# Local attention followed by two expert layers on one core: another order within the attention loop's steps

## Chip, core and metric

The program runs on one NeuronCore of a Trainium2 chip. TensorE (PE in the rows) does matmuls and transposes, VectorE is DVE, ScalarE is ACT, GpSimd is POOL, and SyncE (SP) issues most of the DMA transfers. Each engine works through its own queue in order and waits where an operand is not ready. The metric is the device time of one execution in microseconds; lower is better. All times below are microseconds unless they say ns.

## What is computed

Three layers stand one behind the other: attention with a local window and a few global keys, a layer in which each row goes to one of 8 experts, and a layer in which each row goes through all 4 experts, weighted. Cut to what matters:

```python
# attention: B=2, H=8, S=768, D=64, n_global=8, n_local=96
scores = q @ k.T / sqrt(D) + bias            # kept only for global keys and the last 96 positions
a = exp(scores - max(scores)); a /= sum(a) + 1e-9
x = (a @ v).reshape(1536, 512)
# first expert layer: 1 of 8 per row, chosen by the largest logit
logits = normalized(x) @ normalized(emb).T / tau
e = argmax(logits);  y = gate * (relu(x @ w1[e]) @ w2[e])
# second expert layer: all 4
out = sum_e p[:, e] * (relu(y @ v1[e]) @ v2[e])
```

## The kernel before

**Tiles and runs.** The 1536 rows are 12 tiles of 128 (index `t_`), 6 per batch element. The 8 heads of a tile are 4 pairs (index `n` runs over all tiles' pairs), and two pairs are a *run*. The attention loop makes 24 steps `s_` (line 565); step `s_` belongs to tile `s_ // 2`, its first or second run (`i` = 0 or 1). In a tile at the start of a batch element the scores are 128 columns wide, elsewhere 240.

**What a run goes through.** `scores` (4 matmuls in the program, 8 records in the trace, line 474) into two PSUM buffers, one for each head of a pair, both pairs side by side; `maximum` on VectorE (485: adds the bias in place and takes the row maximum, followed by a small read of the accumulator); `expo` on ScalarE (493: exponential into `aa`, row sum into `sums`); `flip` (501: transposes of `aa` on TensorE, then a copy to `ats`, 503, on ScalarE or VectorE); `av` (515: matmuls with the values into `o`); `fin0` (193: copy of half a tile's `o` to `os` on ScalarE); `fin_l` (210: matmuls of `os` with an identity that also holds the expert embedding, into the single PSUM buffer `l`, tile name `lp`); then on VectorE `over_sums` (229, `lh`) and `rows_x` (241, `xall`), which multiply by the reciprocal of the sums that `sum_up` makes (219 on GpSimd, 220 on VectorE).

**Routing.** When both runs of a tile are there, `choose` queues five closures with six small VectorE operations (257 to 260, 252, 253) that find the expert; `fill()` takes one closure out of that queue. `count` (269, 270) counts with two small matmuls where each row goes, `fin2` (278 to 284) turns that into a slot number, and `scatter` (289, GpSimd's DMA queue) writes the tile's rows into the DRAM buffer `xs`, which `zero_fill` (420) has set to zero in four transfers.

**Order.** The order is written out by hand: every engine executes what the Python code issues to it, in that order, and waits are put in for the data and the buffers. In step `s_` the code issues, in this order: the flips of the step's own run, `ends(s_)` (the end of run `s_ - 2`: `fin_l`, `over_sums`, `rows_x`, and after a second run `fin2` of the tile before and `choose`), `scores(s_ + 2)`, `av` of run `s_ - 1`, then maxima and exponentials of run `s_ + 2` with one `fill()` after each and `fin0` in their midst, then scatter, loads, zero rows and the first expert layer's weights (`load_to`, `split_to`).

**The end of attention.** After the loop, `scatter` of tile 9, then SP loads the first expert's rows `xe` from `xs` (622); they are turned by 16 matmuls (299, `first_rows`), the last two tiles' rows are added by `add_rows` (303) with a permutation that `fin2` makes (281), and the result is split in `x0` (650, 651). Then the first expert's matmuls start (798).

Of the kernel before, what the change touches and what calls it, by code (L numbers as in the profile page):

```python
# [34 lines left out]
def tile_attention_moe_moe(ctx: ExitStack, tc: tile.TileContext, q, k, v, n_global, n_local,  # L35
# [179 lines left out]
    def sum_up(t_):  # L215

        rs = pl.sb.tile([P, H], F32, tag="rs", name="rs")
        lh = pl.sb.tile([P, H, NE], F32, tag="lh", name="lh")
        nc.gpsimd.tensor_scalar(rs, sums[t_], 1e-9, None, ALU.add)
        nc.vector.reciprocal(rs, rs)  # L220
        osb[t_, 2] = rs, lh

    def over_sums(t_, i):
# [82 lines left out]
    with ExitStack() as at:  # L306
# [144 lines left out]

        sc, nm_, aa, ats = {}, {}, {}, {}
        NS = 2 * T

        def pairs(s_):
            return range(2 * s_, 2 * s_ + 2)
# [30 lines left out]
        def expo(n, j):  # L487
            t_, p_ = divmod(n, NP)
            w = P if t_ % TB == 0 else WIN
            if j == 0:  # L490
                aa[n] = ap4.tile([P, 2, 2 * P], F32, tag="aa", name="aa")
            h = 2 * p_ + j
            nc.scalar.activation(aa[n][:, j, 0:w], score(n, j), AF.Exp, bias=nm_[t_][:, h:h + 1], scale=-1.0,  # L493
                                 accum_out=sums[t_][:, h:h + 1])
# [29 lines left out]
        def ends(s_):  # L524

            t_, i = divmod(s_ - 2, 2)
            if t_ >= 0:
                fin_l(t_, i, place=t_ - 1 if i and t_ else None)
                if i == 0:
                    sum_up(t_)  # L530
                over_sums(t_, i)
                rows_x(t_, i)
                if i:
                    if t_:
                        fin2(t_ - 1)
                    choose(t_)

        warm(10)
        build_bias0(0)
# [6 lines left out]
        warm(4)  # L546
        for n in pairs(0):
            for j in range(2):
                maximum(n, j)
                expo(n, j)  # L550
        build_bias0(2)
        build_bias0(3)
        for n in pairs(1):
            for j in range(2):
                maximum(n, j)
                expo(n, j)
        build_biasw(0)
        build_biasw(1)
        nc.gpsimd.memset(zt, 0.0)
        nc.gpsimd.memset(idn[:, :, 2 * D:], 0.0)  # L560
        nc.gpsimd.tensor_copy(idn[:, :, 0:2 * D], ident.unsqueeze(1).to_broadcast([P, NP, P]))
# [3 lines left out]
        for s_ in range(NS):  # L565
            t_, i = divmod(s_, 2)
            n0, n1 = pairs(s_)
            flip(n0, nc.scalar.copy)
            flip(n1, nc.scalar.copy if s_ % 2 else nc.vector.tensor_copy)
            ends(s_)  # L570
            if s_ == 1:
                build_enblk2()
            if s_ == 23:
                break
            scores(s_ + 2)
            if s_ >= 1:
                for n in pairs(s_ - 1):
                    av(n)
            if s_ == 0:
                build_biasw(2)  # L580
                build_biasw(3)
                build_enblk()
            for n in pairs(s_ + 2):
                for j in range(2):
                    if n < NP * T:
                        maximum(n, j)
                        expo(n, j)
                    fill()
                    if s_ >= 1 and n % 2 == 1 and j == 0:
                        fin0((s_ - 1) // 2, (s_ - 1) % 2)  # L590
            if s_ == 1:
                put_globals(0, 1, TB - 1)
            if s_ == 2 * TB - 2:
                put_globals(1, 0, TB - 1)
            if s_ == 2:
                build_flag()
            if ready:
                scatter(ready.pop(0))
            if i == 0 and 1 <= t_ and t_ + 2 < T:
                load_v(t_ + 2)  # L600
            if i == 1 and t_ + 4 < T:
                load_kq(t_ + 4)
            if s_ == 1:
                build_tables()
            if s_ == 4:
                ci = ap1.tile([P, CAP], I32, name="ci")
                nc.gpsimd.iota(ci, [[1, CAP]], base=0, channel_multiplier=0)
                nc.gpsimd.tensor_copy(col, ci)
            if s_ < 4:
                zero_fill(s_)  # L610
            if i == 1:
                load_to(min(nxt[1] + RAW, t_))
                if t_ >= 1:
                    split_to(min(t_ - 1, PRE - 2))
            else:
                split_low(nc.gpsimd, False)


        scatter(ready.pop(0))
        xe = ap1.tile([P, 2, NP, P], F32, name="xe").rearrange("p i a n -> p i (a n)")  # L620
        for i in range(2):
            nc.sync.dma_start(out=xe[:, i], in_=xs[i * P:(i + 1) * P, :])
        for n in pairs(NS - 2):
            av(n)
        fin0(T - 1, 0)
        for n in pairs(NS - 1):
            av(n)
        fin0(T - 1, 1)
# [1 line left out]
        fin_l(T - 1, 0, place=T - 2)  # L630
        fin2(T - 2)
        scatter(ready.pop(0))
        sum_up(T - 1)
        over_sums(T - 1, 0)
        rows_x(T - 1, 0, True)
        fin_l(T - 1, 1, ps_a)
# [389 lines left out]
    with tc.If(fb > 0):  # L1026
        with ExitStack() as ge:
# [23 lines left out]
            for b in range(B):  # L1051
                og = gp.tile([P, TB, NP, P], F32, tag="og", name="og")
                sg = gp.tile([P, TB, H], F32, tag="sg", name="sg")
                for p_ in range(NP):
                    gq = gp.tile([P, TB, P], F32, tag="gq", name="gq")
                    gk = gp.tile([P, S], F32, tag="gk", name="gk")
                    gv = gp.tile([P, TB, 2 * D], F32, tag="gv", name="gv")
                    nc.sync.dma_start(out=gq, in_=q[b * TB:(b + 1) * TB, :, p_, :].rearrange("t p s -> p t s"))
                    nc.sync.dma_start(out=gk, in_=k[b, :, p_, :])
                    nc.sync.dma_start(out=gv, in_=v[b, :, p_ * 2 * D:(p_ + 1) * 2 * D].rearrange("(t s) d -> s t d", s=P))  # L1060
                    for i in range(TB):
                        po = ps_g.tile([P, P], F32, tag="po", name="po")
                        for j in range(2):
                            h = 2 * p_ + j
                            r0 = slice(64 * j, 64 * j + 64)
                            sg_ = gp.tile([P, S], F32, tag="s", name="s")
                            for f in range(2):
                                pt = ps_g.tile([P, S // 2], F32, tag=f"sc{f}", name="pt")
                                cs = slice(f * S // 2, (f + 1) * S // 2)
                                nc.tensor.matmul(pt, gq[r0, i, :], gk[r0, cs], start=True, stop=True)  # L1070
                                nc.vector.scalar_tensor_tensor(sg_[:, cs], dist[:, i, cs], -8.0 * 2.0 ** (-8.0 * (h + 1) / H), pt,
                                                               ALU.mult, ALU.add)
                            kp = keep[:, i, :]
                            nc.vector.tensor_tensor(sg_, sg_, kp, ALU.mult)
                            mk = gp.tile([P, S], F32, tag="mk", name="mk")
                            nc.vector.tensor_scalar(mk, kp, -1.0, NEG8, ALU.add, ALU.mult)
                            nc.vector.tensor_tensor(sg_, sg_, mk, ALU.add)
                            nm = gp.tile([P, 1], F32, tag="nm", name="nm")
                            nc.vector.tensor_reduce(nm, sg_, AX.X, ALU.max)
                            nc.vector.tensor_scalar(nm, nm, -0.125, None, ALU.mult)  # L1080
                            nc.scalar.activation(sg_, sg_, AF.Exp, bias=nm, scale=0.125, accum_out=sg[:, i, h:h + 1])
                            for c in range(TB):
                                pt = ps_g.tile([P, P], F32, tag="at", name="pt")
                                nc.tensor.transpose(pt, sg_[:, c * P:(c + 1) * P], ident)
                                at_ = gp.tile([P, P], F32, tag="at", name="at")
                                nc.vector.tensor_copy(at_, pt)
                                nc.tensor.matmul(po[r0, :], gv[:, c, j * D:(j + 1) * D], at_, start=c == 0, stop=c == TB - 1)
                        nc.vector.tensor_copy(og[:, i, p_, :], po)
                for i in range(TB):
                    t_ = b * TB + i  # L1090
                    sums[t_] = sg[:, i, :]
                    osb[t_] = og[:, i]
                    sum_up(t_)
                    for j in range(2):
                        fin_l(t_, j)
                        over_sums(t_, j)
                        rows_x(t_, j)
                    choose(t_)
                    fill(len(small))
# [104 lines left out]
```

## Time and profile before

| | |
|---|---|
| runs | 840.21, 841.39, 841.75 (median 841.39) |
| the profiled execution | 841.09, of which the span of the trace is 839.4 |
| busy in the span | PE 801.0 (95%), DVE 548.3 (65%), ACT 355.8 (42%), POOL 269.1 (32%) |
| attention, until the first expert's first matmul | 0 to 130.1 |
| the two expert layers | 130.1 to 839.4 |
| DMA | 77.8 MB, 93 GB/s over the span |

Read the shares stage by stage: in the expert layers TensorE is busy all the time, in attention none of the engines is. So the first question for attention is not which engine has the most work but which chain of waits closes from one step to the next. A row of the chain of waits gives start, length, engine, what it wrote and its line; a row of the timeline gives the same with shapes and, in brackets, the idle time before it and what ended it.

### The profile page before, as it was taken

The page shows a single profiled execution, that of the slowest core. Times are in us where ns is not written, and L with a number is a line of the kernel's source. Part 1 is how long each engine was busy: PE and PEld are TensorE (multiplying, and loading weights), DVE is VectorE, ACT ScalarE, POOL GpSimd, SP SyncE. Part 2 cuts the span into 40 slices and gives each one's busy share as a digit, 9 for nine tenths or more (in the row PEclk, how much of TensorE's full clock was granted, in tenths as well). Part 3 has the DMA queues.
Part 4 walks back from the last instruction along what each step waited for, and adds up shares of the span by engine and source line. Part 5 has one row for each costly group of instructions (what it writes and reads, how often), then busy time and mean ns, then how long its engine had stood idle before and what let it go on. Part 6 is the DMA issues. An engine that isn't in the chain of part 4 may idle for free.

```text
span 839.4 us, 14797 instructions
## 1 busy us (share of the span) xinstructions
PE 801.0 (95%) x5699; PEld 728.8 (87%) x5699; DVE 548.3 (65%) x1358; ACT 355.8 (42%) x733; POOL 269.1 (32%) x248
## 2 busy tenths in 40 slices
PE   7887879999999999999999999999999999999996
PEld 3675668999999998999989989989989989989995
DVE  7667745676666554555676676676676676676674
ACT  5687635775555544354233223224223223223221
POOL 3154126107000025136136136136136235235322
PEclk7999999999999999999999999999999999999998
DMA  8756313666666551001001101110110010000111
GB/s 275 270 185 234 122 64 113 218 202 209 207 205 179 195 186 66 26 26 52 26 26 36 39 27 27 36 40 26 28 50 26 27 51 26 27 1 1 51 51 54
DMA packets 32271, 77.80 MB, mean 93 GB/s; under 512 B 3960, under 2 KB 10120, under 8 KB 32192
## 3 DMA queue, kind: packets, MB, share of 16 engines
q1 hardware_dynamic: 29632, 70.36, 26.5%
q0 software_dynamic: 2416, 6.41, 2.1%
q8 instruction: 47, 0.77, 0.4%
q14 instruction: 32, 0.26, 0.1%
q10 hardware_dynamic: 144, 0.00, 0.0%
HBM read 66.22 MB, written 10.53 MB: 91 GB/s over the span
## 4 chain that ended last, share of the span: by engine, by line
PE 79%; DVE 12%; ACT 5%; issue 2%; DMA 1%; POOL 1%; SPq 0%; POOLq 0%; ACTq 0%; DVEq 0%
PE h L925 9%; PE h L924 9%; PE h L926 9%; PE z L989 8%; PE z L992 8%; PE z L991 8%; PE h L798 4%; PE h L799 4%; PE h L800 4%; PE y L814 4%; PE y L813 4%; PE y L812 4%; ACT aa L493 3%; DVE sh L960 2%; PE lp L210 2%
## 5 line engine op out<-in xcount | busy, mean ns | idle before, releaser
L895 DVE SCALAR_TENSOR_TENSOR xall<-z,rsb,xall 128x256 f32<-128x256 f32 x312 | 133.7, 477 | 35.6 <-PE z L992 35.2
L924 PE MATMUL h<-x2h,wh 128*128 128x512 f32 (+1 forms) x400 | 152.8, 382 | 0.0
L925 PE MATMUL h<-x2l,wh 128*128 128x512 f32 (+1 forms) x400 | 152.8, 382 | 0.0
L926 PE MATMUL h<-x2h,wl 128*128 128x512 f32 (+1 forms) x400 | 152.2, 381 | 0.0
L989 PE MATMUL z<-wt,sh 128*128 128x256 f32 x384 | 109.6, 286 | 4.8 <-DVE xall L895 4.8
L992 PE MATMUL z<-wt,sl 128*128 128x256 f32 x384 | 108.7, 283 | 0.7 <-DVE sl L969 0.7
L991 PE MATMUL z<-wt,sh 128*128 128x256 f32 x384 | 108.6, 283 | 0.0
L941 POOL TENSOR_TENSOR bl<-h,bh 128x512 fp32r<-128x512 f32 (+1 forms) x25 | 31.9, 1274 | 192.6 <-PE z L992 167.5
L956 ACT ACTIVATE ah<-h 128x512 fp32r<-128x512 f32 (+1 forms) x50 | 29.1, 582 | 140.6 <-PE h L926 140.6
L926 PEld LDWEIGHTS h<-x2h,wl 128*128 128x128 f32 x400 | 75.2, 188 | 14.7
L924 PEld LDWEIGHTS h<-x2h,wh 128*128 128x128 f32 x400 | 75.4, 189 | 13.2
L925 PEld LDWEIGHTS h<-x2l,wh 128*128 128x128 f32 x400 | 75.4, 189 | 13.0 <-issue 0.3
L989 PEld LDWEIGHTS z<-wt,sh 128*128 128x128 f32 x384 | 73.5, 191 | 7.7 <-DVE xall L895 6.8
L992 PEld LDWEIGHTS z<-wt,sl 128*128 128x128 f32 x384 | 73.5, 191 | 0.9 <-DVE sl L969 0.9
L991 PEld LDWEIGHTS z<-wt,sh 128*128 128x128 f32 x384 | 73.6, 192 | 0.8
L934 ACT ACTIVATE h<-h 128x512 f32<-128x512 f32 (+1 forms) x50 | 28.7, 574 | 107.3 <-PE h L926 107.3
L91 DVE TENSOR_TENSOR wl<-raw,wh 128x1024 fp32r<-128x1024 f32 x61 | 74.0, 1234 | 0.0
L812 PE MATMUL y<-hh,wh 128*128 128x256 f32 x256 | 73.2, 286 | 0.0
L814 PE MATMUL y<-hh,wl 128*128 128x256 f32 x256 | 72.0, 281 | 0.0
L813 PE MATMUL y<-hl,wh 128*128 128x256 f32 x256 | 71.9, 281 | 0.0
L110 ACT ACTIVATE wh<-raw 128x1024 fp32r<-128x1024 f32 x66 | 69.0, 1056 | 2.9 <-DMA raw<-in_moe_w_dram 2.9
L152 POOL TENSOR_TENSOR wt<-raw,wt 128x512 fp32r<-128x512 f32 x40 | 51.6, 1299 | 57.4 <-ACT wt L151 50.2
(214 smaller groups left out, 1987.5 us busy)
## 6 DMA issues: line engine op xcount, KB each, us to landing
raw<-in_moe_w_dram SPq DMA_DIRECT2D x96, 512.0 KB, 3.7
xs<-zt SPq DMA_DIRECT2D x4, 1024.0 KB, 5.8
xr<-xs SPq DMA_DIRECT2D x14, 256.0 KB, 4.0
k<-in_k_dram SPq DMA_DIRECT2D x12, 256.0 KB, 3.4
q<-in_q_dram SPq DMA_DIRECT2D x12, 256.0 KB, 5.1
v<-in_v_dram SPq DMA_DIRECT2D x12, 256.0 KB, 2.8
vwin<-in_v_dram SPq DMA_DIRECT2D x10, 192.0 KB, 4.2
xe<-xs SPq DMA_DIRECT2D x2, 256.0 KB
```

The lines of the kernel that those rows point to most:

```text
L91: eng.tensor_tensor(lo, r, hi.bitcast(F32), ALU.subtract)
L110: nc.scalar.activation(hi, r, AF.Copy)
L812: nc.tensor.matmul(y_, wh[:, f, ws], hh[:, kf, :], start=kf == 0, stop=False)
L813: nc.tensor.matmul(y_, wh[:, f, ws], hl[:, kf, :], start=False, stop=False)
L814: nc.tensor.matmul(y_, wl[:, f, ws], hh[:, kf, :], start=False, stop=kf == KF - 1)
L895: nc.vector.scalar_tensor_tensor(a_, src[:, i], w_, a_, ALU.mult, ALU.add)
L924: nc.tensor.matmul(pt, wh[:, d, ws], x2h[:, d, cs], start=d == 0, stop=False)
L925: nc.tensor.matmul(pt, wh[:, d, ws], x2l[:, d, cs], start=False, stop=False)
L926: nc.tensor.matmul(pt, wl[:, d, ws], x2h[:, d, cs], start=False, stop=d == KD - 1)
L989: nc.tensor.matmul(pt[:, i], hh[:, f, ts_], wh[:, f, :], start=o_ < 3 and i == f == 0, stop=False, skip_group_check=True)
L991: nc.tensor.matmul(pt[:, i], hh[:, f, ts_], wl[:, f, :], start=False, stop=False, skip_group_check=True)
L992: nc.tensor.matmul(pt[:, i], hl[:, f, ts_], wh[:, f, :], start=False, stop=f == 1, skip_group_check=True)
```

## The change

All of it is in the attention loop and its end.

- Within a step the order is now: maxima and exponentials of run `s_ + 1` (`top`, mixed with the flips of run `s_`), `ends(s_)`, `av` of run `s_ - 1`, `fin0`, all waiting small operations at once (`fill(len(small))`), and last `scores(s_ + 2)`. So the scores made at the end of a step are taken up in the following step.
- The flips' copies swap: ScalarE makes both in even steps, VectorE one in odd steps.
- `sum_up`'s reciprocal is issued in `ends`, its GpSimd part at the end of the odd step before.
- `count` and `fin2` of the tile before go with a tile's first run, and no longer with the second.
- Zero rows are written in steps 2, 4, 5 and 7, scatters begin in step 9, one per step while any are ready. The load of `xe` is issued in step 22, inside the loop.

```diff
@@ sum_up
-        nc.vector.reciprocal(rs, rs)
@@ ends
-                fin_l(t_, i, place=t_ - 1 if i and t_ else None)
                 if i == 0:
-                    sum_up(t_)
+                    nc.vector.reciprocal(osb[t_, 2][0], osb[t_, 2][0])
+                fin_l(t_, i, place=t_ - 1 if t_ and not i else None)
                 over_sums(t_, i)
                 rows_x(t_, i)
                 if i:
-                    if t_:
-                        fin2(t_ - 1)
                     choose(t_)
+                elif t_:
+                    fin2(t_ - 1)
+
+        def top(n, j):
+            if n < NP * T:
+                maximum(n, j)
+                expo(n, j)
@@ the loop
+            m0, m1 = pairs(s_ + 1)
+            top(m0, 0)
             flip(n0, nc.scalar.copy)
-            flip(n1, nc.scalar.copy if s_ % 2 else nc.vector.tensor_copy)
-            ends(s_)
+            top(m0, 1)
+            flip(n1, nc.vector.tensor_copy if s_ % 2 else nc.scalar.copy)
+            top(m1, 0)
+            top(m1, 1)
...
+            ends(s_)
-            scores(s_ + 2)
             if s_ >= 1:
                 for n in pairs(s_ - 1):
                     av(n)
...
-            for n in pairs(s_ + 2):
-                for j in range(2):
-                    if n < NP * T:
-                        maximum(n, j)
-                        expo(n, j)
-                    fill()
-                    if s_ >= 1 and n % 2 == 1 and j == 0:
-                        fin0((s_ - 1) // 2, (s_ - 1) % 2)
+                fin0((s_ - 1) // 2, (s_ - 1) % 2)
+            fill(len(small))
+            scores(s_ + 2)
+            if i:
+                sum_up(t_)
...
-            if ready:
+            if ready and s_ > 8:
                 scatter(ready.pop(0))
...
-            if s_ < 4:
-                zero_fill(s_)
+            if s_ in ZF:
+                zero_fill(ZF.index(s_))
...
-        scatter(ready.pop(0))
-        xe = ap1.tile([P, 2, NP, P], F32, name="xe").rearrange("p i a n -> p i (a n)")
-        for i in range(2):
-            nc.sync.dma_start(out=xe[:, i], in_=xs[i * P:(i + 1) * P, :])
-        for n in pairs(NS - 2):
-            av(n)
-        fin0(T - 1, 0)
+            if s_ == NS - 2:
+                xe = ap1.tile([P, 2, NP, P], F32, name="xe").rearrange("p i a n -> p i (a n)")
+                for c in range(2):
+                    nc.sync.dma_start(out=xe[:, c], in_=xs[c * P:(c + 1) * P, :])
```

Before the loop, maxima and exponentials of run 1 and part of the bias tables move into its first steps.

What stands in a row on ScalarE over two steps in the middle of the loop. Before (`aa` is an exponential, `ats` a flip's copy, `os` the copy of `fin0`):

```order
L493 ACTIVATE aa,sums<-s,nm 128x240
L503 COPY ats<-at 128x512 x2
L493 ACTIVATE aa,sums<-s,nm 128x240 x3
L193 COPY os<-o 128x256
L493 ACTIVATE aa,sums<-s,nm 128x240
L503 COPY ats<-at 128x512
L493 ACTIVATE aa,sums<-s,nm 128x240 x3
L193 COPY os<-o 128x256
```

The same two steps after the change, the even one first:

```order
L493 ACTIVATE aa,sums<-s,nm 128x240
L503 COPY ats<-at 128x512
L493 ACTIVATE aa,sums<-s,nm 128x240
L503 COPY ats<-at 128x512
L493 ACTIVATE aa,sums<-s,nm 128x240 x2
L193 COPY os<-o 128x256
L493 ACTIVATE aa,sums<-s,nm 128x240
L503 COPY ats<-at 128x512
L493 ACTIVATE aa,sums<-s,nm 128x240 x3
L193 COPY os<-o 128x256
```

A flip's copy now stands between the first and the second exponential of a run, and `os` behind all four.

VectorE before, from the end of `fin2` to the next reciprocal (`s,nm` with its `nm` row is one maximum, `l`, `sm`, `oh`, `ohb` are the small operations of `choose`):

```order
L485 ISA s,nm<-s,biasw 128x240
L485 ISA nm 128x1
L257 TENSOR_REDUCE l_79<-lh 128x8
L485 ISA s,nm<-s,biasw 128x240
L485 ISA nm 128x1
L258 TENSOR_REDUCE sm<-l_79 128x1
L485 ISA s,nm<-s,biasw 128x240
L485 ISA nm 128x1
L259 SCALAR_TENSOR_TENSOR sm<-l_79,sm,rev 128x8
L485 ISA s,nm<-s,biasw 128x240
L485 ISA nm 128x1
L260 TENSOR_REDUCE sm<-sm 128x1
```

VectorE after, from the last maximum of an odd step:

```order
L485 ISA s,nm<-s,biasw 128x240
L485 ISA nm 128x1
L228 TENSOR_TENSOR lh<-lp,rs 128x32
L240 TENSOR_TENSOR xall<-lp,rs 128x256
L256 TENSOR_REDUCE l_79<-lh 128x8
L257 TENSOR_REDUCE sm<-l_79 128x1
L258 SCALAR_TENSOR_TENSOR sm<-l_79,sm,rev 128x8
L259 TENSOR_REDUCE sm<-sm 128x1
L251 TENSOR_SCALAR oh<-sm 128x8
L252 CAST ohb<-oh 128x8
```

The six small operations, spread over the maxima before, now stand in one row behind `xall`, and the next step's first maximum behind them.

GpSimd's queue at the end of attention, before:

```order
L289 DMA xs<-xall,slot 2048x512
L254 TENSOR_TENSOR cum<-cum,oh 128x8
L285 TENSOR_TENSOR base<-pos 128x1
L289 DMA xs<-xall,slot 2048x512
L219 TENSOR_SCALAR rs<-sums 128x8
L254 TENSOR_TENSOR cum<-cum,oh 128x8
```

and after:

```order
L288 DMA xs<-xall,slot 2048x512
L253 TENSOR_TENSOR cum<-cum,oh 128x8
L219 TENSOR_SCALAR rs<-sums 128x8
L284 TENSOR_TENSOR base<-pos 128x1
L288 DMA xs<-xall,slot 2048x512
L253 TENSOR_TENSOR cum<-cum,oh 128x8
```

The sums `rs` of the last tile stood behind the scatter of tile 10; now they stand ahead of it.

## Rows read from the trace of the kernel before

**Rows 1.** Busy time by stretch: length, PE, PEld, DVE, ACT, POOL, PEclk, DMA share.

```profile
140.00:160.00 20.00, 20.00 (x171) 20.00 (x171) 13.49 (x21) 14.14 (x30) 9.05 (x12) 1.00 0.72 234
```

**Rows 2.** Chain of waits, 0 to 215: start, length, engine, written, line.

```profile
23.84 0.40 DVE s L485
...
82.89 0.76 PE lp L210 x4
83.65 1.06 PE s L474 x8
...
87.24 0.76 PE lp L210 x4
...
91.80 0.76 PE lp L210 x4
...
110.38 1.03 PE o L515 x16
111.40 1.02 PE at L501 x8
112.43 0.49 PE lp L210 x4
...
114.06 0.22 DVE slot L284
```

**Rows 3.** Timeline of two steps, 82 to 91.5: start, length, engine, line.

```profile
87.08 0.47 ACT L493 ACTIVATE aa<-s,nm 128x240 f32<-128x240 f32 x1
...
87.53 1.08 ACT L503 COPY ats<-at 128x512 f32<-128x512 f32 x2
...
88.11 0.19 DVE L229 TENSOR_TENSOR lh<-lp,rs 128x32 f32<-128x32 f32 x1 [1.18 <-PE lp L270]
...
88.54 0.16 DVE L278 CUSTOM_DVE_ANT_0 g<-ebase,oh 128x8 f32<-128x8 f32 x1
...
89.14 0.22 DVE L284 SCALAR_TENSOR_TENSOR slot<-pos 128x1 int32<-128x1 f32 x1
...
89.28 0.41 DVE L485 CUSTOM_DVE_ANT_0 s<-s,biasw 128x240 f32<-128x240 f32 x1
...
89.60 0.26 DVE L257 TENSOR_REDUCE l<-lh 128x8 f32<-128x64 f32 x1
...
89.84 0.46 ACT L493 ACTIVATE aa<-s,nm 128x240 f32<-128x240 f32 x1 [1.23 <-DVE nm L485]
...
90.42 0.42 DVE L485 CUSTOM_DVE_ANT_0 s<-s,biasw 128x240 f32<-128x240 f32 x1 [0.16 <-ACT aa L493]
```

**Rows 4.** Timeline of the end of attention, 104 to 132.

```profile
107.09 0.41 DVE L485 CUSTOM_DVE_ANT_0 s<-s,biasw 128x240 f32<-128x240 f32 x1
...
121.16 3.67 PE L299 MATMUL xy<-ident,xe 128*128 128x128 f32 x16 [4.29 <-DMA xe<-xs]
...
123.85 0.20 DVE L220 RECIPROCAL rs<-rs 128x8 f32<-128x8 f32 x1 [6.47 <-POOL rs L219]
124.09 0.29 DVE L229 TENSOR_TENSOR lh<-lp,rs 128x32 f32<-128x32 f32 x2
...
124.41 0.27 DVE L257 TENSOR_REDUCE l<-lh 128x8 f32<-128x64 f32 x1
...
125.72 0.42 DVE L241 TENSOR_TENSOR xall<-lp,rs 128x256 f32<-128x256 f32 x1
...
125.86 0.17 PE L269 MATMUL pp<-ohb,tri 128*128 128x8 bf16 x1 [0.16 <-DVE ohb L253]
...
130.11 0.38 PE L798 MATMUL h<-x,wh 128*128 128x256 f32 x1 [0.92 <-DVE x L651]
```

**Rows 5.** Busy time by stretch of 2 us, the columns of rows 1.

```profile
118.00:120.00 2.00, 0.00 (x0) 0.00 (x0) 0.00 (x0) 0.00 (x0) 0.00 (x0) 1.00 0.10 30
...
122.00:124.00 2.00, 2.00 (x12) 2.00 (x11) 0.15 (x1) 0.00 (x0) 1.23 (x2) 0.50 0.00 0
```

**Rows 6.** DMA issues on the page: count, KB each, median us to landing.

```profile
xs<-zt SPq DMA_DIRECT2D x4, 1024.0 KB, 5.8
```

More of the change, by code (lines that the diff above doesn't have):

```diff
@@ L453, in tile_attention_moe_moe @@
         NS = 2 * T
+        ZF = (2, 4, 5, 7)
         def pairs(s_):
@@ L548, in tile_attention_moe_moe @@
             for j in range(2):
-                maximum(n, j)
-                expo(n, j)
+                top(n, j)
         build_bias0(2)
         build_bias0(3)
-        for n in pairs(1):
-            for j in range(2):
[L555 to L558, printed above, removed]
         nc.gpsimd.memset(zt, 0.0)
@@ L567, in tile_attention_moe_moe @@
             n0, n1 = pairs(s_)
+            m0, m1 = pairs(s_ + 1)
+            top(m0, 0)
             flip(n0, nc.scalar.copy)
-            flip(n1, nc.scalar.copy if s_ % 2 else nc.vector.tensor_copy)
-            ends(s_)
+            top(m0, 1)
+            flip(n1, nc.vector.tensor_copy if s_ % 2 else nc.scalar.copy)
+            top(m1, 0)
+            top(m1, 1)
+            if s_ < 2:
+                build_biasw(2 * s_)
+                build_biasw(2 * s_ + 1)
+            if s_ == 0:
+                build_enblk()
             if s_ == 1:
                 build_enblk2()
-            if s_ == 23:
-                break
-            scores(s_ + 2)
+            ends(s_)
             if s_ >= 1:
@@ L578, in tile_attention_moe_moe @@
                     av(n)
[L579 to L582, printed above, removed]
-            for n in pairs(s_ + 2):
-                for j in range(2):
-                    if n < NP * T:
-                        maximum(n, j)
-                        expo(n, j)
-                    fill()
-                    if s_ >= 1 and n % 2 == 1 and j == 0:
-                        fin0((s_ - 1) // 2, (s_ - 1) % 2)
+                fin0((s_ - 1) // 2, (s_ - 1) % 2)
[3 more added lines that the diff above has]
+                sum_up(t_)
             if s_ == 1:
@@ L632, in tile_attention_moe_moe @@
         scatter(ready.pop(0))
-        sum_up(T - 1)
+        nc.vector.reciprocal(osb[T - 1, 2][0], osb[T - 1, 2][0])
         over_sums(T - 1, 0)
@@ L1093, in tile_attention_moe_moe @@
                     sum_up(t_)
+                    nc.vector.reciprocal(osb[t_, 2][0], osb[t_, 2][0])
                     for j in range(2):
```

## Prediction

> **What bounds the kernel now.** I read the busy time by stretch first. From 140 on TensorE is busy for the whole of a stretch at full clock [rows 1], and no instruction of the two expert layers changes. So they keep their 709 us (130.11 to 839.4), start when attention ends, and all that can be won or lost lies before the first expert's matmul at 130.11 [rows 4].
>
> The chain of waits comes next, because no engine is full in attention. In the loop it returns to the same instruction, `fin_l`'s matmuls: 82.89, 87.24, 91.80 [rows 2], which is 8.91 for a pair of steps. TensorE's own work in a step is 1.02 (transposes), 1.03 (`o`), 1.06 (`s`) and 0.49 (`lp` where it didn't have to wait) [rows 2], 3.60 in all, 7.2 for a pair, and the two small counting matmuls. So 1.5 to 1.7 of each 8.91 is waiting. The loop closes like this: `lp`, behind it the scores, from them the maxima, the exponentials, in their midst `os` on ScalarE, and `os` feeds the next `lp`. One run goes nearly all the way round in each step.
>
> The timeline gives the hand-offs that any order has to pay. From a maximum to its exponential 0.56 (89.28 to 89.84), and from that exponential to the third maximum of the run 0.58 (89.84 to 90.42), which waits for ScalarE although it belongs to another pair [rows 3]: both lie in one PSUM buffer. The fourth waits for the second exponential in the same way.
>
> **The change, part by part. The loop.** The scores of a run are now made a step before they are needed, and `lp` comes behind 1.02 of transposes, so the old ring is cut open. What ring is late next? In the new order VectorE does four maxima, then the end of an older run, then the next step's maxima. The fourth maximum needs the second exponential, and on ScalarE a flip's copy now stands between the first and the second. So I go from the first maximum of one step to that of the next, with durations from the rows:
>
> maximum to exponential 0.56; exponential to copy 0.45 (87.08 to 87.53); copy 0.54 (half of 1.08); second exponential to fourth maximum 0.58 [rows 3]. Together 2.13 in every step. The fourth maximum to the instruction behind it takes 0.32 (89.28 to 89.60).
>
> Even step, then: reciprocal to `lh` 0.24 (123.85 to 124.09) [rows 4], `lh` to `fin2` 0.43 (88.11 to 88.54), `fin2` to its `slot` 0.60, `slot` to the next maximum 0.14 [rows 3]. 2.13 + 0.32 + 0.24 + 0.43 + 0.60 + 0.14 = 3.86.
>
> Odd step: `lh` and `xall` 0.43 again, and the six small operations in one row 1.31 (124.41 to 125.72) [rows 4]. Spread over the maxima they were nearly free, here they are on the path. 2.13 + 0.32 + 0.43 + 1.31 = 4.19.
>
> A pair takes 8.05 instead of 8.91. Other rings are shorter. TensorE's work is 7.4 for a pair, counting matmuls included. The way exponential, transpose, `lp`, `o`, `s`, maximum goes over two steps: 2.13 to the fourth maximum, 0.56 and some 0.5 for the last exponential, 1.02, 0.49, 1.03 and 1.06, which is 6.8. ScalarE has four exponentials, one or two copies and `os`, some 3.5 in a step, and 1.1 more where a weight is split; that stands behind `os`, ends before the next first exponential, and so stays hidden (if not, one for one).
>
> In the odd steps VectorE's copy stands ahead of the third maximum. It costs nothing while it can start within 1.07 of the first maximum (2.13 less 0.46 and 0.54 and a little), and the transposes that it needs should be done 0.3 after it.
>
> From the first maximum of run 4 (23.84) [rows 2] to that of run 23 (107.09) [rows 4] it was 83.25 for 19 steps, 1.4 less than 19 halves of 8.91, since one tile's runs are narrow. Now it is 10 odd steps of 4.19 and 9 even ones of 3.86, 76.64; for the narrow runs I take off 1.0. 75.6, a gain of 7.6. How the hand-offs add up where they have never stood together is unknown: 0.15 less for a pair or 0.45 more, so 9.0 down to 3.3.
>
> **The first steps.** The same bias tables, maxima and copies stand on VectorE up to run 4, only in another order, and VectorE works there nearly without a break. I take 0, with 0.7 either way: below, because zero rows no longer compete with the first keys and queries; above, because copies now delay maxima.
>
> **Zero rows, scatters, loads.** Four transfers of 1 MB land 5.8 after their issue [rows 6]. SP issues the last in step 7, the first scatter waits for it in GpSimd's queue at the end of step 9, some 8 later. Behind a scatter that waits would stand `cum` and the sums `rs`, which VectorE needs at the end of step 12: another 12 of cover, then one for one. The first weights are queued behind zero rows on SP, with about 8 from issue to use; late ones would hold ScalarE. I take 0, and at most 1 lost.
>
> **The end.** The `xe` load is issued a step earlier, and what follows it is the old chain. Before, `slot` at 114.06 [rows 2], through scatter and load, led to the first turning matmul at 121.16; from there 4.70 to the counting matmul (125.86), and 4.25 to the expert's first matmul (130.11). Counted from the first maximum of run 23 at 107.09 that is 23.02 [rows 4]. Now that maximum stands in step 22, an even one, whose `slot` comes 3.86 - 0.14 = 3.72 later: 3.72 + 7.10 + 4.70 + 4.25 = 19.77. The gain is 3.25. The last run's flips, `av`, `fin0` and `lp` are done about 8 after that maximum, inside the 7.10; the last tile's expert is known at about 11, behind `rs`, which no longer waits in GpSimd's queue behind a scatter that waits for `xe` (the 6.47 of idle time at 123.85) [rows 4]. That wait was hidden behind TensorE and is not counted again.
>
> Of the 4.70, 3.67 are 16 matmuls at half clock [rows 4]: TensorE had no work from 118 to 120, with the full clock still granted (1.00), and at 122 to 124 it had 0.50, 1.2 GHz [rows 5]. At full clock the turning takes 2.04 (twice 1.02 of 8 transposes [rows 2]), and the rest a few tenths less, so the end would gain 5.2. Now TensorE will be without work for about 3 instead of 4.3. I take half clock, the nearest row. The Trainium skill, "TensorE: Matmul & The Clock Gate", section "Part 1: The HAM clock gate", says that the slow clock is the default and that only activity lifts it. By that alone every such pause ends at half clock and the time is the 830.5 below; by the row in which the clock outlasted the pause it would be 828.5.
>
> **The sum.** 7.6 + 0 + 0 + 3.25 = 10.9 off the profiled execution's 841.09 is 830.2. That execution was 0.3 under the median of 841.39, so against the runs I say 830.5.
>
> **Rivals.**
> *TensorE becomes the bound.* If the third and fourth maximum don't have to wait behind the copy, a pair takes TensorE's 7.4: 1.5 x 9.5 = 14.3, less 0.5 for narrow runs, and 3.25: 824.3. For it speaks that TensorE's share is already the largest; against it the wait of 0.16 on ScalarE that the trace shows for just this maximum [rows 3].
> *The loop doesn't open.* The step stays at 4.45 because hand-offs grow, or `lp`, of which there is one buffer, is held by a late `fin2`; only the end is won: 838.1. For it: half of the new ring is small VectorE operations, whose price is taken from two places at the end of attention. Against it: the ring is made of measured steps throughout.
> *Slower: the copy blocks VectorE.* In odd steps the copy stands in VectorE's queue ahead of the third and fourth maxima, the end of the older run and the next step's maxima. It needs the second transposes, these need the fourth exponential of the even step. If they are ready only after 1.07 from the first maximum, each 0.1 more costs 0.1 a pair, 0.95 in all; from 2.2 on the loop's and the end's gain is gone, and at 2.5 the pair costs 1.43 more than my 8.05, 13.6 in all: 844.1. Against it: by my sum the transposes are ready some 0.8 before that point. For it: such a copy at the head of an in-order queue ties all three engines together.
>
> **Chances.** Forecast, 826 to 835.5: 0.62. TensorE bound: 0.09. The loop stays, 835.5 to 839: 0.19. Slower by the copy or by late weights: 0.10. The range reaches from the forecast's lower end to most of the third case: 826 to 837. About 0.2%, 1.7 us, is what a measurement of this kernel can tell from no change. Faster by more than that 0.86, within it 0.05, slower 0.09.
>
> **What would show it.** The distance of `lp` to `lp` over two steps should be 8.0 to 8.2, odd steps 0.3 longer than even ones; the fourth maximum should wait for ScalarE, no longer the first for TensorE; TensorE should wait before the second flip for an exponential. `xe` should be issued some 8 after the first maximum of run 23, and the expert's first matmul should stand at about 119. I am wrong if the pair stays near 8.9, if maxima wait for TensorE's scores, if ScalarE waits for a weight's transfer, or if the experts take longer than 709.

## Result and profile after

| | before | after |
|---|---|---|
| median of the runs | 840.99 (840.21 to 841.75) | 833.22 (831.79 to 833.34) |
| the profiled execution, of which span | 841.09, 839.4 | 833.17, 831.5 |
| first maximum of run 4 (`maximum`) | 23.84 | 22.54 |
| first maximum of run 23 | 107.09 | 103.66 |
| first expert's first matmul | 130.11 | 122.46 |

The ratio is 0.9904 [0.9887, 0.9921]: 7.8 faster, inside the range of 826 to 837, but 2.7 short of the 830.5. By stretch, in the two profiled executions:

| stretch | forecast gain | measured gain |
|---|---|---|
| up to the first maximum of run 4 | 0 | 1.30 |
| from there to the first maximum of run 23 | 7.6 | 2.13 (83.25 to 81.12) |
| from there to the expert's first matmul | 3.25 | 4.22 (23.02 to 18.80) |
| the expert layers | 0 | 0.3 |
| sum | 10.9 | 7.9 |

So the total came nearer than its terms, partly by luck: the loop lost 5.5 of what it should have won, and two stretches gave back 2.3 unasked. What happened in the loop stands in the chain of waits of the changed kernel (start, length, engine, written, line):

```profile
38.54 2.37 DVE slot L283
...
48.73 2.38 DVE slot L283
...
62.23 0.75 DVE sm L258
...
69.94 0.71 DVE sm L258
...
78.46 0.51 DVE sm L258
```

The `slot` of the kernel before is in the same view with 0.22 [rows 2]: one VectorE instruction on a 128x1 column has become eleven times as long. The timeline of the changed kernel shows what else is going on then (start, length, engine, line, operation, in brackets the idle time before and what ended it):

```profile
48.54 0.15 DVE L282 TENSOR_SCALAR pos<-pos 128x1 f32<-128x1 f32 x1
48.59 0.19 POOL L284 TENSOR_TENSOR base<-pos 128x1 f32<-128x1 f32 x1 [3.05 <-DVE pos L278]
48.73 2.38 DVE L283 SCALAR_TENSOR_TENSOR slot<-pos 128x1 int32<-128x1 f32 x1
48.73 2.36 POOL L91 TENSOR_TENSOR wl<-raw,wh 128x1024 fp32r<-128x1024 f32 x1
...
51.03 0.40 DVE L485 CUSTOM_DVE_ANT_0 s<-s,biasw 128x240 f32<-128x240 f32 x1
...
51.60 0.46 ACT L493 ACTIVATE aa<-s,nm 128x240 f32<-128x240 f32 x1 [2.94 <-DVE nm L485]
```

`wl` is the low half of a weight's split, which GpSimd makes in even steps from step 6 on (`split_low`, five times in the loop). `slot` starts with it and ends with it, and the exponentials wait 2.94 behind it. In steps 6 and 8 `wl` stands right behind `base`. From step 10 on a scatter (1.01 in the row below) stands between them, `wl` starts that much later and meets `sm` of the odd step instead:

```profile
59.54 1.01 POOL L288 DMA_INDIRECT xs<-xall,slot  x1 [0.17 <-issue]
...
60.56 2.38 POOL L91 TENSOR_TENSOR wl<-raw,wh 128x1024 fp32r<-128x1024 f32 x1
...
61.41 0.41 DVE L240 TENSOR_TENSOR xall<-lp,rs 128x256 f32<-128x256 f32 x1
61.74 0.26 DVE L256 TENSOR_REDUCE l<-lh 128x8 f32<-128x64 f32 x1
...
62.04 0.16 DVE L257 TENSOR_REDUCE sm<-l 128x1 f32<-128x8 f32 x1
62.23 0.73 DVE L258 SCALAR_TENSOR_TENSOR sm<-l,sm,rev 128x8 f32<-128x8 f32 x1
```

`xall` and two reductions run at their usual length beside `wl`, and the next instruction, `sm`, stands still until `wl` ends at 62.94. Over an undisturbed 0.22 or 0.24 the long rows are 2.15, 2.16, 0.51, 0.47 and 0.27 too long; with 0.24 on `slot` at 58.92, beside a GpSimd copy of 0.45, that is 5.8. In the kernel before no `slot` and no `sm` is longer than 0.23: there `wl`, as long as here, runs beside maxima and ends before `slot` starts (timeline of the kernel before):

```profile
42.20 2.35 POOL L91 TENSOR_TENSOR wl<-raw,wh 128x1024 fp32r<-128x1024 f32 x1
...
45.84 0.22 DVE L284 SCALAR_TENSOR_TENSOR slot<-pos 128x1 int32<-128x1 f32 x1
```

Outside these places the ring is what was forecast. Three first maxima in the undisturbed part of the changed kernel, and between the last two the fourth maximum of an even step (89.65):

```profile
83.41 0.41 DVE L485 CUSTOM_DVE_ANT_0 s<-s,biasw 128x240 f32<-128x240 f32 x1
...
87.58 0.41 DVE L485 CUSTOM_DVE_ANT_0 s<-s,biasw 128x240 f32<-128x240 f32 x1
...
89.65 0.42 DVE L485 CUSTOM_DVE_ANT_0 s<-s,biasw 128x240 f32<-128x240 f32 x1 [0.46 <-ACT aa L493]
...
91.46 0.41 DVE L485 CUSTOM_DVE_ANT_0 s<-s,biasw 128x240 f32<-128x240 f32 x1
```

4.17 for an odd step (87.58 less 83.41), 3.88 for an even one, 8.05 for a pair; the sums were 4.19, 3.86 and 8.05.

### The profile page after: what moved, and what is told of

Read it like the earlier page. It is cut to its first block, busy times and chain, and to the rows that moved or that the text cites. A ratio compares the mean times of both kernels' runs of the same rounds, so it can differ in the third digit from the quotient of the medians.

```text
span 831.5 us, 14790 instructions
## 1 busy us (share of the span) xinstructions
PE 801.4 (96%) x5699; PEld 726.3 (87%) x5699; DVE 555.3 (67%) x1358; ACT 354.0 (43%) x733; POOL 268.6 (32%) x248
## 4 chain that ended last, share of the span: by engine, by line
PE 76%; DVE 14%; ACT 5%; issue 2%; DMA 1%; POOL 0%; ACTq 0%; DVEq 0%; POOLq 0%; SPq 0%
PE h L919 9%; PE h L920 9%; PE h L921 9%; PE z L984 9%; PE z L987 8%; PE z L986 8%; PE h L793 4%; PE h L795 4%; PE h L794 4%; PE y L809 4%; PE y L808 4%; PE y L807 4%; ACT aa L493 3%; DVE sh L955 2%; DVE s L485 2%
```

## Experiments

**The theory:** a VectorE instruction that takes two tensors from SBUF stands still while GpSimd reads SBUF for `wl`. `slot` (`pos`, `pos`) and `sm` (`l`, `rev`) are such instructions; the maxima take one tensor from PSUM and one from SBUF, `xall` too. **Rivals:** the long rows are waits for data, for a buffer or for a transfer; or any small VectorE instruction on SBUF is held up. The Trainium skill, "SBUF — State Buffer", section "SBUF: two separate sides", states the theory's rule: VectorE and GpSimd share a pair of SBUF ports under an exclusive lock, it is contended by a VectorE instruction with two SBUF inputs against a GpSimd instruction that reads SBUF (and by a VectorE instruction in a two-port mode, which no run here tests), and whoever starts first keeps it for the whole instruction. The runs below bear on its two conditions, the second input and the reading.

| label | median (range) | ratio to before |
|---|---|---|
| the change | 833.22 (831.79 to 833.34) | 0.9904 [0.9887, 0.9921] |
| e1_split_behind_sums | 828.11 (826.07 to 829.04) | 0.9845 [0.9831, 0.9858] |
| e2_dose_read | 837.99 (836.73 to 839.15) | 0.9965 [0.9954, 0.9977] |
| e3_dose_write | 832.31 (830.94 to 833.21) | 0.9902 [0.9886, 0.9917] |
| e4_zero_rows_early | 833.37 (831.82 to 834.93) | 0.9911 [0.9897, 0.9925] |
| f3_slot_one_tensor | 829.03 (827.16 to 829.16) | 0.9849 [0.9834, 0.9864] |
| g2_scatters_early | 828.86 (828.05 to 830.42) | 0.9848 [0.9829, 0.9867] |
| f1_ring | 820.39 (820.05 to 822.33) | 0.9751 [0.9736, 0.9766] |
| f2_full_clock | 826.40 (825.88 to 827.59) | 0.9824 [0.9809, 0.9839] |
| f5_ring_full_clock | 821.70 (819.96 to 823.02) | 0.9766 [0.9749, 0.9783] |
| g1_weight_ahead | 819.62 (817.98 to 819.89) | 0.9732 [0.9712, 0.9752] |

### The split moved out of the way

```diff
-            if ready and s_ > 8:
-                scatter(ready.pop(0))
...
                 if t_ >= 1:
                     split_to(min(t_ - 1, PRE - 2))
-            else:
-                split_low(nc.gpsimd, False)
+                    split_low(nc.gpsimd, False)
+            if ready and s_ > 8:
+                scatter(ready.pop(0))
```

> GpSimd's split of a weight (wl, 128x1024, 2.35) moves from the even step, where it starts beside the end of fin2, to the odd step directly behind the split on ScalarE, ahead of the scatter, so that it runs beside the next step's maxima. Theory (VectorE's instructions with two SBUF inputs stand still while GpSimd reads SBUF for wl): no slot or sm longer than 0.3 in steps 6 to 15, first maximum of run 4 to first maximum of run 23 at 75.3 to 76.0 instead of 81.1, time 833.2 - 5.8 = 827.4. Rival (the long slot and sm rows are waits for data, buffers or a DMA that the profile draws into the instruction): moving wl leaves 833.2, and long rows stay in the same steps. Rival (wl blocks the maxima as much): long rows move to the maxima, 833.

Measured 828.1, 5.1 less. The loop takes 76.08 (22.41 to 98.49). No `sm` is long any more and no `slot` stands still for `wl`, though `wl` is as long as ever; it now runs beside maxima (timeline of this kernel, step 6):

```profile
35.25 2.37 POOL L91 TENSOR_TENSOR wl<-raw,wh 128x1024 fp32r<-128x1024 f32 x1
...
35.83 0.42 DVE L485 CUSTOM_DVE_ANT_0 s<-s,biasw 128x240 f32<-128x240 f32 x1 [0.31 <-ACT aa L493]
...
37.50 0.41 DVE L240 TENSOR_TENSOR xall<-lp,rs 128x256 f32<-128x256 f32 x1
...
38.43 0.22 DVE L283 SCALAR_TENSOR_TENSOR slot<-pos 128x1 int32<-128x1 f32 x1
```

Neither rival fits: the data are the same, and neither maxima nor `xall` became longer under `wl`. Two rows stayed long. One `slot` (at 54.58) takes 0.45 and ends with a scatter of GpSimd. And in one step of a narrow run `wl` reaches into `fin2`: its `g`, another operation with two tensors from SBUF (`ebase`, `oh`), takes 0.50 in place of 0.16 and ends with `wl`:

```profile
59.32 2.37 POOL L91 TENSOR_TENSOR wl<-raw,wh 128x1024 fp32r<-128x1024 f32 x1
...
61.20 0.50 DVE L277 CUSTOM_DVE_ANT_0 g<-ebase,oh 128x8 f32<-128x8 f32 x1
```

### A dose that reads and a dose that only writes

```diff
                 elif t_:
                     fin2(t_ - 1)
+                    if s_ in (16, 18, 20):
+                        z2 = zt.unsqueeze(1).to_broadcast([P, 2, DM])
+                        nc.gpsimd.tensor_tensor(dz, z2, z2, ALU.add)
```

> Behind base of fin2 in steps 16, 18 and 20, which are undisturbed, GpSimd adds a tile of zeros to itself (128x1024, reads and writes SBUF, an estimate of 2.4 each from wl). Nothing waits for the result. Theory (lock while GpSimd reads SBUF): slot takes 2.3 instead of 0.22 in these three steps, +6.3 in all, 839.5. Rival (a data wait): nothing on VectorE depends on it, 833.2. Both expect the scatters 2.4 later in GpSimd's queue, without effect on the end.

In the other kernel three `nc.gpsimd.memset(dz, 0.0)` stand there instead.

> The same places as in the run with the added reads, but GpSimd only writes there: three memsets of 128x1024, some 2.6 in all (an estimate from the memset of 128x7168 at 6.1). Theory with the lock on GpSimd's reads alone: slot stays 0.22, 833.2. Rival (any GpSimd instruction on SBUF blocks VectorE): slot takes the first memset's length, 0.9 to 1.0, +2.1 to 2.4 in all, 835.5.

The timeline with the reading dose:

```profile
83.18 1.92 DVE L283 SCALAR_TENSOR_TENSOR slot<-pos 128x1 int32<-128x1 f32 x1
83.19 1.89 POOL L540 TENSOR_TENSOR dz<-zt 128x1024 f32<-128x1024 f32 x1
```

and with the writing one:

```profile
83.20 0.95 POOL L539 MEMSET dz<- 128x1024 f32 x1
83.22 0.22 DVE L283 SCALAR_TENSOR_TENSOR slot<-pos 128x1 int32<-128x1 f32 x1
```

An addition whose result nobody needs makes `slot` as long as itself, three times: 3 x 1.70 = 5.1 expected from the rows, 4.8 measured (837.99 less 833.22). My 839.5 was too high because I took 2.4 for the addition's length, which is 1.89. GpSimd writing for 0.95 changes nothing. A wait for data cannot produce the first result, and a hold by any GpSimd instruction cannot produce the second.

### One tensor less on VectorE

```diff
-        nc.vector.scalar_tensor_tensor(slot[:, t_:t_ + 1], pos[:, 1:2], pos[:, 0:1], pos[:, 2:3], ALU.add, ALU.add)
+        nc.vector.tensor_scalar(slot[:, t_:t_ + 1], pos[:, 1:2], pos[:, 0:1], pos[:, 2:3], ALU.add, ALU.add)
```

> The changed kernel (833.2), its weight split where the change has it, but slot is made by a tensor_scalar with one tensor input and two per-partition scalars in place of a scalar_tensor_tensor with two tensor inputs. Theory (only a second tensor input from SBUF is locked out): slot takes 0.2 in steps 6, 8 and 10 although wl runs beside it, 2.15 + 2.16 + 0.24 less; the sm rows of 0.5 to 0.75 stay; 828.7 to 829.3. Rival (every small VectorE instruction on SBUF, or any with per-partition scalars from SBUF, stands still while wl runs): slot stays at 2.37, 833.2.

```profile
38.22 0.27 DVE L283 TENSOR_SCALAR slot<-pos 128x1 int32<-128x1 f32 x1
38.23 2.36 POOL L91 TENSOR_TENSOR wl<-raw,wh 128x1024 fp32r<-128x1024 f32 x1
38.41 0.41 DVE L485 CUSTOM_DVE_ANT_0 s<-s,biasw 128x240 f32<-128x240 f32 x1
```

The same three columns from SBUF, two of them as per-partition scalars: `slot` takes 0.27 beside `wl`, and the time is 829.0, 4.2 less, as expected from the lock. So it is the second tensor input that is locked out, not smallness and not SBUF as such. With the two doses this shows both conditions of the skill's rule. That whoever starts first keeps the ports is shown for GpSimd first only (`sm`, 1.67 behind the start of `wl`); in the `slot` rows both start within 0.01, and no run has such a VectorE instruction clearly ahead.

### Zero rows and scatters as before the change

```diff
-        ZF = (2, 4, 5, 7)
+        ZF = (0, 1, 2, 3)
```

> The four zero fills go back to steps 0 to 3, everything else as in the changed kernel. Theory (the 1.3 that the first steps won came from the keys and queries that no longer compete with zero rows): the first maximum of run 4 goes from 22.5 back to 23.5 to 24, time 834.2 to 834.7. Rival (the new order of flips, maxima and scores in the first steps won it): it stays at 22.5 and the time at 833.2. The long slot and sm rows stay in both.

833.4, no difference, and the first maximum of run 4 stands at 22.25. My theory for the first steps fell. In this execution TensorE has the half clock there, as in the kernel before, and it costs nothing. The zero rows alone don't bring it: in g2_scatters_early, which writes them in the same steps and moves as many bytes in the same stretch, the granted clock is 1.00 (busy time by stretch, of e4_zero_rows_early and then of g2_scatters_early: length, PE, PEld, DVE, ACT, POOL, PEclk, DMA share, GB/s):

```profile
16.00:18.00 2.00, 2.00 (x10) 1.29 (x11) 1.76 (x8) 1.87 (x8) 0.11 (x2) 0.50 1.06 390
16.00:18.00 2.00, 2.00 (x19) 1.27 (x15) 1.72 (x7) 1.90 (x10) 0.41 (x3) 1.00 1.06 387
```

In the kernel before VectorE waited for TensorE three times in the first steps (timeline of the kernel before):

```profile
19.17 0.42 DVE L485 CUSTOM_DVE_ANT_0 s<-s,biasw 128x240 f32<-128x240 f32 x1 [0.35 <-PE s L474]
...
22.13 0.69 DVE L503 COPY ats<-at 128x512 f32<-128x512 f32 x1 [0.84 <-PE at L501]
...
23.82 0.42 DVE L485 CUSTOM_DVE_ANT_0 s<-s,biasw 128x240 f32<-128x240 f32 x1 [0.27 <-PE s L474]
```

Together 1.46. With the scores a step ahead, neither the changed kernel nor this one shows such a wait. That fits the 1.3; no run isolates it further.

The second kernel also lets scatters begin with the first tile (`if ready:` in place of `if ready and s_ > 8:`).

> The changed kernel (833.2) with zero rows in steps 0 to 3 and scatters from the first tile on, as before the change; the order within the steps stays changed. Theory (lock): in steps 6 and 8 a scatter of 1.05 now stands between base and wl in GpSimd's queue, wl misses slot and hits sm of the odd step with some 0.5 to 0.75 in place of 2.37; 2 x 1.65 = 3.3 less, 829.9: so much of the loss came from the scatters being begun later. Rival (scatters and loads compete, or the long slot rows have to do with the zero rows' transfers): 833.2 or, with the transfers as before, the first steps 1.3 longer, 834.5.

828.9: by the medians 4.4 less than the change, 1.1 more than expected from the two steps alone. In the profiled executions the loop is 2.9 shorter (81.12 to 78.21). The scatter keeps `wl` from `slot` in steps 6 and 8, and `sm` pays less (timeline):

```profile
39.66 1.07 POOL L288 DMA_INDIRECT xs<-xall,slot  x1 [0.52 <-DVE slot L283]
40.75 2.38 POOL L91 TENSOR_TENSOR wl<-raw,wh 128x1024 fp32r<-128x1024 f32 x1
...
42.59 0.57 DVE L258 SCALAR_TENSOR_TENSOR sm<-l,sm,rev 128x8 f32<-128x8 f32 x1
```

Its five `sm` are 0.53 to 0.92 long, 2.1 too long in all. So of the change's parts, beginning the scatters later, which I had put at nothing, cost 2.9 by the loops and 4.4 by the medians, by taking a spacer out of GpSimd's queue.

### The ring itself

On top of the moved split:

```diff
             top(m0, 0)
-            flip(n0, nc.scalar.copy)
             top(m0, 1)
+            flip(n0, nc.scalar.copy)
```

> On top of the split moved behind the sums (828.1): in each step the second exponential is issued ahead of the first flip's copy on ScalarE. Theory (the step's length is the ring maximum, exponential, copy, second exponential, fourth maximum, small operations): the fourth maximum comes 0.48 earlier (copy 0.58 goes out of the ring, the accumulator read stays), a pair goes from 8.05 to 7.1 by that ring and is then held by TensorE's own work at 7.4 to 7.6; 19 steps give 4.3 to 6.2 less, 822 to 824. Rival (the two engines' work elsewhere, such as the second flip's exponential or os, holds the pair at about 8): within 1 of 828.1.

820.4, by the medians 7.7 less than with the moved split alone: more than my theory's own range, because TensorE didn't hold the pair at 7.4. The timeline, an odd step and an even one:

```profile
75.50 0.41 DVE L485 CUSTOM_DVE_ANT_0 s<-s,biasw 128x240 f32<-128x240 f32 x1
...
76.53 0.45 ACT L493 ACTIVATE aa<-s,nm 128x240 f32<-128x240 f32 x1
...
76.96 0.58 ACT L503 COPY ats<-at 128x512 f32<-128x512 f32 x1
...
77.11 0.45 DVE L485 CUSTOM_DVE_ANT_0 s<-s,biasw 128x240 f32<-128x240 f32 x1
...
79.20 0.41 DVE L485 CUSTOM_DVE_ANT_0 s<-s,biasw 128x240 f32<-128x240 f32 x1
...
82.59 0.41 DVE L485 CUSTOM_DVE_ANT_0 s<-s,biasw 128x240 f32<-128x240 f32 x1
```

A pair takes 7.09 (75.50 to 82.59): the copy's part, 2 x 0.48, is gone from the ring, as its sum says. The fourth maximum (77.11) no longer waits. TensorE's 7.4, the number behind my first rival, was too high by at least 0.3. It is counted as busy for all of the 7.09, but its weight loads still wait up to 0.3 for an exponential; whether it holds the next step down, no run shows.

The shorter steps uncover a transfer. In the profiled execution of this kernel, the slowest of its five (822.33), the split of the second quarter on ScalarE waits for its weight:

```profile
42.20 1.06 ACT L110 ACTIVATE wh<-raw 128x1024 fp32r<-128x1024 f32 x1 [2.62 <-DMA raw<-in_moe_w_dram]
```

One more line loads it a tile earlier:

```diff
-                load_to(min(nxt[1] + RAW, t_))
+                load_to(min(nxt[1] + RAW, t_ + (t_ > 0)))
```

> On top of the run with the ring (820.4): the second quarter of the first weights is loaded one tile earlier, in step 3 in place of step 5, ahead of two zero fills on SyncE's queue. Theory (with the shorter steps the split of that quarter waits 2.0 to 2.6 for its transfer on ScalarE, the exponentials stand behind it, and the loop loses as much): that wait is gone, 818.0 to 818.5. Rival (the keys, queries or zero rows that now come behind the weight are late in their turn, or the wait is covered): 820.4.

In its profile ScalarE waits for no weight, and the loop takes 68.63 (21.77 to 90.40) instead of 71.83. By the medians it is 819.6 against 820.4, with overlapping intervals: the times don't tell the gain from none. The clock at the end, which the next section is about, blurs them: the 16 turning matmuls took 3.34 in this profiled execution and 2.05 in that of f1_ring. Either way this version is 13 to 14 under the change, and the fastest here.

### The clock at the end

On top of the moved split, fourteen matmuls on zeros ahead of the 16 turning ones:

```diff
+        for _ in range(14):
+            nc.tensor.matmul(xy[3], zb[:, 0:P], zb[:, 0:CAP], start=True, stop=True)
         first_rows(xe)
```

> On top of the split moved behind the sums (828.1): 14 matmuls of 128x256 bf16 on zeros, some 1.5 in all, stand on TensorE ahead of the 16 turning matmuls, in the time in which it waits for xe; the turning matmuls overwrite their result. Theory (the half clock of the turning comes from TensorE's idle time ahead of it): the granted clock stays at 1.00, the turning takes 2.05 in each run instead of 2.05 to 3.6, time 826.6, and the runs lie closer together. Rival (the clock falls at the end of attention whatever TensorE does, or the dummies come late): 828.1 or up to 0.5 more.

> Both edits of the two runs above at once, on top of the split moved behind the sums. If both theories hold and don't meet: 828.1 - 5 - 1.5 = 821 to 822.5. If the shorter ring makes the scores and the last run's transposes late at the end, the wait for xe is longer and the 14 matmuls cover less of it: up to 1.5 more.

826.4 against 828.1, as expected, though the ranges overlap (825.88 to 827.59, 826.07 to 829.04); on top of the ring 821.7 against 820.4, no gain. The profiles of f1_ring and of f5_ring_full_clock both have the full clock there, so on the ring these two executions offered nothing to win. Nor does the full clock with the fourteen prove that they kept it, since three kernels without them turned at full clock too (below): their effect isn't shown. With the fourteen, on the moved split, TensorE waits 0.31 and turns at full clock (timeline of f2_full_clock):

```profile
106.84 1.69 PE L636 MATMUL xy<-zb 128*128 128x256 bf16 x14
...
108.56 1.86 PEld L298 LDWEIGHTS xy<-ident,xe 128*128 128x128 f32 x16 [0.31 <-DMA xe<-xs]
108.56 2.05 PE L298 MATMUL xy<-ident,xe 128*128 128x128 f32 x16
```

## Why the prediction held, and where it did not

**The loop's sum** held. Even step 3.86 forecast, 3.88 measured; odd 4.19 and 4.17; loop 75.6, and 76.08 once `wl` is out of the way. The fourth maximum waits for ScalarE, 0.46 in an even step, the first no longer for TensorE. The ring f1_ring cuts is the one that I summed.

**The step that failed** is "Zero rows, scatters, loads", with its "I take 0, at most 1 lost". It went through what the moved scatters and `fin2` wait for, in GpSimd's queue and on SP, and never through what runs beside them. The change moves `fin2` into the even step, in which GpSimd splits a weight, and the later scatters take 1.05 out from between. Its price is 5.8 by the rows and 5.1 by the run without it. With that term the sum would have been some 836; the 2.3 that other stretches gave, which I hadn't counted, bring it to 833.3 to 834. That the total came within 2.7 of 830.5 is luck in this part.

**The first steps**, 0 with 0.7 either way, gave 1.3. I saw VectorE without a break, but three of its waits, 1.46 in all, were for TensorE, and they are gone in the new order.

**The end** gave 4.22 instead of 3.25. `slot` stands 3.74 behind the first maximum of run 23 (3.72 forecast), and `xe` was issued at 111.35, 7.7 behind it. From `slot` to the turning it is 6.82 where I took 7.10, and from there to the expert's matmul 8.24 instead of 8.95. Of these 0.71, 0.36 are two waits of TensorE for VectorE in the kernel before (0.16 for `ohb` [rows 4], 0.20 for `pos` at 127.23), which I took over in 4.70 and 4.25 and which are gone; 0.15 is the shorter turning, and the rest is open.

```profile
107.40 0.22 DVE L283 SCALAR_TENSOR_TENSOR slot<-pos 128x1 int32<-128x1 f32 x1
...
111.35 0.81 SPq L618 DMA_DIRECT2D xe<-xs  x2
...
114.22 3.52 PE L298 MATMUL xy<-ident,xe 128*128 128x128 f32 x16 [2.13 <-DMA xe<-xs]
...
122.46 0.39 PE L793 MATMUL h<-x,wh 128*128 128x256 f32 x1 [0.92 <-DVE x L646]
```

**The half clock** at the turning, for which I had a choice between two rows, is not settled for this kernel. In its profiled execution TensorE turned in 3.52, after 2.13 without work; with the writing dose the same matmuls took 2.05 after 1.65, in f1_ring 2.05 after 1.83, and in f3_slot_one_tensor also 2.05, after 2.00:

```profile
108.00:110.00 2.00, 0.30 (x2) 1.00 0.81 250
110.00:112.00 2.00, 2.00 (x18) 1.00 0.00 0
```

(busy time by stretch of f3_slot_one_tensor, TensorE alone: length, PE, PEclk, DMA share, GB/s). e1_split_behind_sums took 3.62 after 1.82, so the length of the pause doesn't decide alone. I read the clock-gate rule as "every such pause ends at half clock" (the Trainium skill, "TensorE: Matmul & The Clock Gate", section "Part 1: The HAM clock gate"); these rows show pauses that didn't. It is worth about 1.5, as much as the runs of one kernel scatter here.

**The rivals.** The loop opened, so 838.1 is out. TensorE as the bound at 7.4 is out too: in the changed kernel the copy does stand in the ring, and without it the pair goes below 7.4. VectorE's copy in the odd steps blocked nothing; it runs in 0.69 without a wait. The slower case that was real was one that I did not name.

## What to carry to other kernels

When an instruction is moved, ask besides who waits for it what will run beside it on the other engines, GpSimd above all: here, a 0.22 instruction with two SBUF tensors took 2.37 beside a GpSimd subtraction. Such an overlap shows in the timeline as a VectorE row that ends with a GpSimd row, and no wait is printed, since the time lies inside the instruction. Two cures worked here: move the GpSimd work under instructions that read one of their tensors from PSUM, or give the small instruction (128x1) one tensor and per-partition scalars.

Then sum the ring link by link from rows; that sum held to 0.02 in each step, and it named the next edit, the copy between two exponentials, worth as much as the whole change by the medians (7.7 and 7.8).

## What the runs showed of the hardware

- VectorE's SCALAR_TENSOR_TENSOR with two SBUF tensors took 2.37 and 1.92 beside GpSimd instructions of 2.35 and 1.89 that read SBUF, and 0.22 beside a memset of 0.95. A reduction with two SBUF tensors (`g`) took 0.50 in place of 0.16 beside the end of such a subtraction.
- TENSOR_SCALAR with two per-partition scalars from SBUF took 0.27 beside the same 2.36, and maxima with one tensor in PSUM their usual 0.41.
- TensorE's granted clock after a pause of 1.6 to 2.1 was 1.00 in some executions and 0.50 in others of nearly the same code, with 2.05 at full clock, and from 2.7 to 3.6 where the clock fell, for the same 16 matmuls.
